# Attention on one core: the first K load cut in two parts on two DMA queues

## The chip, the cores and the metric

The kernel runs on one core of one Trainium2 chip. The metric is the device time of one execution in microseconds. In these runs the profiled span is about 1.7 us shorter than the time (823.1 beside 824.83 us).

## The reference

```python
B, H, Sq, Sk, D = 16, 32, 192, 1024, 128          # bf16
def reference(q, k, v):
    scale = q.shape[-1] ** -0.5
    scores = jnp.einsum("bhqd,bhkd->bhqk", q, k) * scale
    p = softmax(scores, axis=-1)
    return jnp.einsum("bhqk,bhkd->bhqd", p, v)
```

There are 512 heads. The inputs are 293.6 MB, the output 25.2 MB.

## The kernel before

The kernel takes four heads at a time: 128 groups, three pieces each. K of a group (1 MB) is loaded with 32 keys in each partition, "turned" by VectorE (32x32 transposes), put in order by GpSimd, and used by TensorE (PE) as the stationary operand of the scores. ScalarE takes the exponential; PE multiplies with V; VectorE divides. PE's program is a loop over two groups. K, V and Q have five buffers each, so at the start five K loads can be issued without waiting.

```python
PIECES = ((0, 6), (6, 12), (12, 16))      # which key blocks are in piece 0, 1, 2

@block.sync
def _(e):
    def load_k(x):
        if x >= NKN:
            e.wait_ge(s_kx, 3 * (x - NKN) + 3)
        e.dma_start(kn[:, x % NKN, :],
                    kf[4*x:4*x+4].rearrange("a (j r) d -> (a j) (r d)", r=32).bitcast(U32),
        ).then_inc(s_kn[x % NKN], 16)
    # ... load_v alike
    load_k(0)
    load_k(1)
    load_q(e, 1)
    for n in range(2, NKN):
        load_v(n - 2)
        load_k(n)
        load_q(e, n)
    # ... then as buffers come free

# VectorE
def turn_k(g):                            # piece g = 3 * x + b
    x, b = divmod(g, 3)
    lo, hi = PIECES[b]
    if b == 0:
        dve.wait_ge(s_kn[x % NKN], 16 * (x // NKN + 1))
    # ... transposes kn[.., lo:hi] into kx
turn_k(0)
turn_q(0)
for g in range(1, 5):
    turn_k(g)
turn_q(1)
# ...

# ScalarE
load_q(act, 0)
act.wait_ge(s_one, 1)
act.activation(pt[:, 1] ...)              # a fill that PE waits for before its loop
# ...
```

A piece is a range of key blocks `lo:hi` inside each of four stretches of a partition's row. Piece 0 is therefore 4 stretches of 768 bytes in each partition (384 KB), and the other keys of the group are 4 stretches of 1280 bytes (640 KB).

Of the kernel before, what the change touches and what calls it, by code (L numbers as in the profile page):

```python
# [407 lines left out]
U32 = mybir.dt.uint32  # L408
# [7 lines left out]
PIECES = ((0, 6), (6, 12), (12, 16))  # L416


def _attention_kernel(nc, q, k, v, out):
# [25 lines left out]
    with ExitStack() as outer:  # L445
        redo = outer.enter_context(nc.sbuf_tensor("redo", [1, 1], mybir.dt.int32))

        def sem(name):
            return outer.enter_context(nc.semaphore(name))

        s_set = sem("f_set")
        s_one = sem("f_one")
        s_kn = [sem("f_kn%d" % i) for i in range(NKN)]
        s_qn = [sem("f_qn%d" % i) for i in range(NKN)]
        s_v = [sem("f_v%d" % i) for i in range(NVS)]
# [16 lines left out]
        with ExitStack() as es:  # L472
# [49 lines left out]
            def load_q(e, x):  # L522
                e.dma_start(
                    qn[:, x % NKN, :],
                    qf[4 * x:4 * x + 4].rearrange("a (j u) d -> (a j) (u d)", u=6).bitcast(U32),
                ).then_inc(s_qn[x % NKN], 16)

            hints = {}

            def hint(eng):  # L530
# [2 lines left out]
# [5 lines that stand above are left out]
                    e.dma_start(  # L538
                        kn[:, x % NKN, :],
                        kf[4 * x:4 * x + 4].rearrange("a (j r) d -> (a j) (r d)", r=32).bitcast(U32),  # L540
                    ).then_inc(s_kn[x % NKN], 16)

                def load_v(x):
                    if x >= NVS:
                        e.wait_ge(s_pv, 3 * (x - NVS) + 2 + BLANK)
                    e.dma_start(
                        vs[:, x % NVS, :, :],
                        vf[4 * x:4 * x + 4].rearrange("a (m t) d -> m a (t d)", t=T),
                    ).then_inc(s_v[x % NVS], 16)

                load_k(0)
                load_k(1)
                load_q(e, 1)
                for n in range(2, NKN):
# [3 lines that stand above are left out]
                for n in range(NQ):  # L558
                    if n == NQ // 2:
                        hint(e)  # L560
                    if n + NKN - 2 < NQ:
                        load_v(n + NKN - 2)
                    if n + NKN < NQ:
                        load_k(n + NKN)
                        load_q(e, n + NKN)
                for i in range(len(store_at), len(stores)):
                    store(e, i)
# [125 lines left out]
            @block.vector  # L693
            def _(dve):
                dve.memset(pt[:, 0].rearrange("p a c -> p (a c)").bitcast(U32), 0).then_inc(s_set, 1)  # L695
                dve.sem_inc(s_e1, 1)
                dve.sem_inc(s_e3, 3)
                dve.sem_inc(s_vp, 2)
                dve.sem_inc(s_on, LAG + 1)
                where = {}  # L700
                for i, (x0, c) in enumerate(stores):
                    for a in range(c):
                        where[x0 + a] = (i, a)

                def turn_k(g):
                    x, b = divmod(g, 3)
                    lo, hi = PIECES[b]
                    if b == 0:
                        dve.wait_ge(s_kn[x % NKN], 16 * (x // NKN + 1))
                    if x >= 2:  # L710
                        dve.wait_ge(s_qk, 3 * (x - 2) + b + 1)
                    dve.transpose(  # L712
                        kx[:, x % 2].rearrange("p (U s j u) -> p s u U j", s=2, j=32, u=2)[:, :, :, lo:hi],
                        kn[:, x % NKN].rearrange("p (s u U i) -> p s u U i", s=2, u=2, i=32)[:, :, :, lo:hi],
                    ).then_inc(s_kx, 1)

                def turn_q(x):
                    dve.wait_ge(s_qn[x % NKN], 16 * (x // NKN + 1))
                    if x >= R:
                        dve.wait_ge(s_qk, 3 * (x - R) + 3)  # L720
                    dve.transpose(  # L721
                        qt[:, x % R].bitcast(U32).rearrange("p b (y j u) c -> p u y b (j c)", y=3, u=2),
                        qn[:, x % NKN].rearrange("p (u y b i) -> p u y b i", u=2, y=3, b=2),
                    ).then_inc(s_qt, 1)

                def onorm(s):
                    x, w = divmod(s, 3)
                    i, a = where[x]
                    so = i % NSO
                    ri = rinv[:, 2 * s: 2 * s + 2]  # L730
                    dve.wait_ge(s_pv, s + 1 + BLANK)
                    O = o_of(s)
                    dve.reciprocal(ri, O[:, :, 128]).then_inc(s_rc, 1)  # L733
                    dve.wait_ge(s_rc, s + 1)
                    if a == 0 and w == 0 and i >= NSO:
                        dve.wait_ge(s_st[so], 16 * (i // NSO))
                    dve.tensor_tensor(  # L737
                        ob[:, so, 6 * a + 2 * w: 6 * a + 2 * w + 2, :],
                        O[:, :, 0:128],
                        ri.unsqueeze(2).to_broadcast([128, 2, D]),  # L740
                        ALU.mult,
                    ).then_inc(s_on if s < NF - 1 else s_fin, 1)

                cnt = [0]

                def check(lo, hi, i, part):
                    c = chk[:, lo:hi]
                    if part == 0:
                        ins = dve.tensor_scalar(c, rinv[:, lo:hi], 1.0 / RS_HI, 1.0 / RS_LO, ALU.max, ALU.min)  # L749
                    elif part == 1:  # L750
                        ins = dve.tensor_tensor(c, c, rinv[:, lo:hi], ALU.not_equal)  # L751
                    else:
                        ins = dve.tensor_reduce(bad[:, i: i + 1], c, mybir.AxisListType.X, ALU.max)  # L753
                    ins.then_inc(s_dv, 1)
                    cnt[0] += 1
                    dve.wait_ge(s_dv, cnt[0])
# [6 lines that stand above are left out]
                for f in range(NF + LAG + 1):  # L763
                    s = f - LAG - 1
                    if f == NF // 2:
                        hint(dve)
                    if s >= 0:
                        onorm(s)
                        if 0 <= s - EARLY < 3:
                            check(0, 2 * EARLY, 0, s - EARLY)  # L770
                    g = f + 5
                    if g < NF:
                        x, b = divmod(g, 3)
                        if b == 2 and x >= 2:
                            turn_q(x)
                        turn_k(g)
                for part in range(3):
                    check(2 * EARLY, 2 * NF, 1, part)
                dve.sem_inc(s_fl, 1)  # L779
                dve.wait_ge(s_fl, 2)  # L780
                dve.tensor_copy(redo[0:1, 0:1], o_ps[0:1, 0, 0:1]).then_inc(s_fl, 1)  # L781
                dve.wait_ge(s_fl, 3)

            @block.scalar
            def _(act):
                load_q(act, 0)
                act.wait_ge(s_one, 1)
                act.activation(pt[:, 1].rearrange("p a c -> p (a c)").bitcast(F32), ones[:, 0:1].to_broadcast([128, 2 * T * SQ]),  # L788
                               ACT_FN.Copy).then_inc(s_set, 1)
                for f in range(NF):  # L790
                    x, b = divmod(f, 3)
                    if f == NF // 2:
                        hint(act)
                    act.wait_ge(s_qk, f + 1)
                    if 0 < 3 * x + b and b < 2:
                        act.wait_ge(s_pv, 3 * (x - R) + 2 + b + BLANK)
                    c = slice(512 * b, 512 * b + 512)
                    act.activation(pt[:, x % R, 0, c], s1_ps[:], ACT_FN.Exp, scale=scale).then_inc(s_e1, 1)  # L798
                    if b == 0:
                        act.wait_ge(s_pf, x + 1)  # L800
                    act.activation(pt[:, x % R, 1:4, c], s3_ps[f % 2][:], ACT_FN.Exp, scale=scale).then_inc(s_e3, 1)  # L801
                    if f in store_at:
                        store(act, store_at[f])
# [40 lines left out]
```

## Time and profile before

| | |
|---|---|
| Time, first three runs | 823.41 us median (823.04 to 824.85) |
| PE busy over the span | 98% |
| PE from 35 us to the end of the loop | busy (99.96 us of 100 from 200 us on, all of every other stretch), one group each 6.21 us |
| First scores | 8.62 us |
| DMA | 400 to 405 GB/s |

The first lines are the page's own: busy time of the engines, and two rows of the 40 slices (granted TensorE clock and DMA share in tenths).

```profile
PE 807.8 (98%) x32926; PEld 717.7 (87%) x32926; DVE 599.6 (73%) x1288; ACT 748.5 (91%) x770; POOL 549.6 (67%) x646
...
PEclk9899999999999999999999999999999999999999
DMA  9999999999999999999999999999999999999961
```

The next are two stretches of the table of windows (stretch, its length, busy time of each engine with its instructions, clock, DMA share, GB/s). They show that PE leaves no gap in the steady part. A change of the start can therefore only move this steady part as a whole.

```profile
60.00:100.00 40.00, 40.00 (x1642) 35.71 (x1644) 29.84 (x64) 37.42 (x40) 27.34 (x33) 1.00 1.04 405
400.00:500.00 100.00, 100.00 (x4126) 89.25 (x4120) 74.73 (x161) 93.63 (x98) 68.23 (x81) 1.00 1.04 401
```

The timeline of the start follows: start, duration, engine, line, operation, count, and in brackets the engine's idle time and what ended it. It shows the chain from the load to the first scores (6.43, 7.47, 8.62), and then three stalls of PE inside runs of matmuls where the program has no wait (2.41, 3.06 and 2.12 us; "issue" means that the profile shows nothing that PE waited for).

```profile
0.80 0.40 ACTq L523 DMA_DIRECT2D f_qn<-in_q_dram  x1
...
0.81 0.89 SPq L538 DMA_DIRECT2D f_kn<-in_k_dram  x2
...
6.43 0.98 DVE L712 STREAM_TRANSPOSE f_kx<-f_kn 128x768 uint32<-128x768 uint32 x1 [2.29 <-DMA f_kn<-in_k_dram]
7.33 0.54 DVE L721 STREAM_TRANSPOSE f_qt<-f_qn 128x384 uint32<-128x384 uint32 x1
...
7.47 0.85 POOL L583 COPY f_kt<-f_kx 128x768 uint32<-128x768 uint32 x1 [2.80 <-DVE f_kx L712]
...
8.62 1.10 PE L628 MATMUL f_s<-f_qt,f_kt 32*128 32x192 bf16 x48 [2.32 <-PEq L611]
...
15.49 0.98 PE L628 MATMUL f_s<-f_qt,f_kt 32*128 32x128 bf16 x40 [2.41 <-issue]
...
21.87 1.62 PE L650 MATMUL f_o<-f_vp,f_pt 128*64 128x129 bf16 x26 [3.06 <-issue]
...
28.46 1.89 PE L628 MATMUL f_s<-f_qt,f_kt 32*128 32x128 bf16 x46 [2.12 <-issue]
```

The last is the DMA view of 2.5 to 4.5 us, when the first loads are moved: queue, packets, MB, share of 16 engines. q1 is SyncE's queue (K), q10 ScalarE's (Q). A packet here is one contiguous run of a load, as the trace records it. There are nearly equal counts of 8 KB and 1.5 KB packets: the two queues take turns. (The records don't name the DMA engine of a packet, so this is read from the counts.)

```profile
DMA packets 145, 0.68 MB, mean 341 GB/s; under 512 B 0, under 2 KB 76, under 8 KB 76
...
q1 hardware_dynamic: 69, 0.57, 68.8%
q10 hardware_dynamic: 76, 0.12, 22.9%
```

### The profile page before, as it was taken

How to read it: one execution, taken by the hardware profiler on the slowest of the kernel's cores; microseconds unless marked ns; L12 is line 12 of the kernel's file. 1: busy time of each engine (PE TensorE's matmuls, PEld its weight loads, DVE VectorE, ACT ScalarE, POOL GpSimd, SP SyncE). 2: the span in 40 equal slices, each digit the busy share in tenths (PEclk: the TensorE clock that was granted, in tenths of full speed). 3: DMA queues.
4: the chain of work that ended last, by engine and by line, in shares of the span. 5: the costliest groups of instructions: out<-in, count | busy, mean ns of one | idle time of the engine just before them, and what ended most of it. 6: DMA issues, size and time to landing. Idle time of an engine off the chain costs nothing. (4 is left out here: it accounts for less than half of the span.)

```text
span 823.1 us, 71558 instructions
## 1 busy us (share of the span) xinstructions
PE 807.8 (98%) x32926; PEld 717.7 (87%) x32926; DVE 599.6 (73%) x1288; ACT 748.5 (91%) x770; POOL 549.6 (67%) x646
## 2 busy tenths in 40 slices
PE   6899999999999999999999999999999999999998
PEld 4788888888888888888888888888888888888887
DVE  5477777777777777777777777777777777777775
ACT  5699999999999999999999999999999999999996
POOL 6466676676676666767667667667666666766762
PEclk9899999999999999999999999999999999999999
DMA  9999999999999999999999999999999999999961
GB/s 355 401 403 406 407 403 407 403 402 404 405 401 394 405 402 402 402 401 391 406 403 399 404 404 394 404 405 397 400 407 395 403 400 402 401 405 401 399 226 59
DMA packets 138293, 319.14 MB, mean 388 GB/s; under 512 B 7184, under 2 KB 56336, under 8 KB 121872
## 3 DMA queue, kind: packets, MB, share of 16 engines
q1 hardware_dynamic: 105376, 294.22, 91.3%
q10 hardware_dynamic: 32880, 24.58, 8.9%
q14 instruction: 32, 0.26, 0.1%
q8 instruction: 5, 0.08, 0.0%
HBM read 293.60 MB, written 25.17 MB: 387 GB/s over the span
## 5 line engine op out<-in xcount | busy, mean ns | idle before, releaser
L801 ACT ACTIVATE f_pt<-f_s 128x1536 bf16<-128x1536 f32 x384 | 554.9, 1445 | 3.2 <-PE f_o L650 3.2
L583 POOL COPY f_kt<-f_kx 128x768 uint32<-128x768 uint32 (+1 forms) x384 | 293.5, 784 | 254.4 <-DVE f_kx L712 134.2
L628 PE MATMUL f_s<-f_qt,f_kt 32*128 32x192 bf16 (+2 forms) x20480 | 422.9, 226 | 6.9 <-issue 4.5
L650 PE MATMUL f_o<-f_vp,f_pt 128*64 128x129 bf16 x12336 | 424.7, 222 | 3.3 <-issue 3.3
L650 PEld LDWEIGHTS f_o<-f_vp,f_pt 128*64 128x64 bf16 x12336 | 365.2, 110 | 54.3 <-issue 24.8
L628 PEld LDWEIGHTS f_s<-f_qt,f_kt 32*128 32x128 bf16 x20480 | 348.2, 92 | 43.2 <-issue 7.4
L712 DVE STREAM_TRANSPOSE f_kx<-f_kn 128x768 uint32<-128x768 uint32 (+1 forms) x384 | 334.1, 871 | 8.7 <-DMA f_kn<-in_k_dram 8.7
L798 ACT ACTIVATE f_pt<-f_s 128x512 bf16<-128x512 f32 x384 | 229.2, 597 | 63.1 <-PE f_s L628 32.9
L592 POOL COPY f_vp<-f_vs 128x1024 uint32<-128x1024 uint32 x256 | 259.1, 1040 | 8.4 <-PE f_o L650 8.4
L733 DVE RECIPROCAL f_rinv<-f_o 128x2 f32<-128x2 f32 x381 | 64.8, 170 | 195.9 <-PE f_o L650 195.9
L737 DVE TENSOR_TENSOR f_ob<-f_o,f_rinv 128x256 bf16<-128x256 f32 x381 | 161.6, 424 | 13.3 <-DVE f_rinv L733 0.3
L721 DVE STREAM_TRANSPOSE f_qt<-f_qn 128x384 uint32<-128x384 uint32 x128 | 72.8, 569 | 0.0
L675 PE MATMUL f_o<-f_ones 128*128 128x512 bf16 x12 | 4.4, 540 | 1.1 <-POOL f_ones L574 1.1
L675 PEld LDWEIGHTS f_o<-f_ones 128*128 128x128 bf16 x12 | 1.5, 131 | 3.5 <-issue 2.2
L575 POOL MEMSET f_vp<- 128x4352 uint32 x1 | 3.7, 3728 | 0.0
L695 DVE MEMSET f_pt<- 128x3072 uint32 x1 | 2.6, 2618 | 1.5 <-PEq L829 1.5
L650 PE MATMUL f_s<-f_vp,f_pt 128*64 128x129 bf16 x96 | 3.1, 220 | 0.4 <-PEq L611 0.4
L650 PEld LDWEIGHTS f_s<-f_vp,f_pt 128*64 128x64 bf16 x96 | 2.8, 110 | 0.5 <-issue 0.5
L788 ACT ACTIVATE f_pt<-f_ones 128x3072 f32<-128x3072 bf16 x1 | 2.8, 2762 | 0.0
L788 ACT ACT_TABLE_LOAD x1 | 1.3, 1283 | 1.2 <-PEq L829 1.2
L733 DVE RECIPROCAL f_rinv<-f_s 128x2 f32<-128x2 f32 x3 | 0.5, 171 | 1.4 <-PE f_s L650 1.4
L689 PE MATMUL f_o<-f_bad,f_ones 128*1 128x1 bf16 x1 | 0.2, 164 | 1.3 <-DVEq L779 1.3
(13 smaller groups left out, 5.3 us busy)
## 6 DMA issues: line engine op xcount, KB each, us to landing
f_kn<-in_k_dram SPq DMA_DIRECT2D x128, 1024.0 KB, 10.6
f_vs<-in_v_dram SPq DMA_DIRECT2D x128, 1024.0 KB, 8.4
f_qn<-in_q_dram SPq DMA_DIRECT2D x127, 192.0 KB, 10.5
out_dram<-f_ob ACTq DMA_DIRECT2D x62, 384.0 KB, 9.5
out_dram<-f_ob SPq DMA_DIRECT2D x1, 384.0 KB, 3.2
out_dram<-f_ob SPq DMA_DIRECT2D x2, 192.0 KB, 2.3
f_qn<-in_q_dram ACTq DMA_DIRECT2D x1, 192.0 KB, 5.0
```

The source lines that it names most:

```text
L583: gp.tensor_copy(kt[:, x % NKT].bitcast(U32).rearrange("p U (j s u) c -> p U j s (u c)", s=2, u=2)[:, lo:hi], kx[:, x % 2].rearrange("p (U ...
L592: gp.tensor_copy(vp[:, x % NVP, 2 * T * i: 2 * T * i + 2 * T, 0:D].bitcast(U32), vs[:, x % NVS, 2 * i: 2 * i + 2, :].rearrange("p a (t d) ...
L628: ins = pe.matmul(S[:, c0: c0 + n1 - n0], kt[r, x % NKT, 2 * t + h, :, c], qt[r, x % R, h, n0:n1, c], start=w == 0 and g == 0, stop=w == 3 ...
L650: return pe.matmul(O[m0: m0 + m, u, 0:129], pt[:, x % R, 2 * y + z, t * SQ + n0: t * SQ + n0 + m], vp[:, x % NVP, (2 * y + z) * T + t, 0:129],
L675: pe.matmul(o_ps[:].rearrange("p a b -> p (a b)"), ones[:], ones[:].unsqueeze(1).to_broadcast([128, 4, 128]), start=True, stop=True)
L712: dve.transpose(kx[:, x % 2].rearrange("p (U s j u) -> p s u U j", s=2, j=32, u=2)[:, :, :, lo:hi], kn[:, x % NKN].rearrange("p (s u U i) ...
L721: dve.transpose(qt[:, x % R].bitcast(U32).rearrange("p b (y j u) c -> p u y b (j c)", y=3, u=2), qn[:, x % NKN].rearrange("p (u y b i) -> ...
L733: dve.reciprocal(ri, O[:, :, 128]).then_inc(s_rc, 1)
L737: dve.tensor_tensor(ob[:, so, 6 * a + 2 * w: 6 * a + 2 * w + 2, :], O[:, :, 0:128], ri.unsqueeze(2).to_broadcast([128, 2, D]), ALU.mult,). ...
L788: act.activation(pt[:, 1].rearrange("p a c -> p (a c)").bitcast(F32), ones[:, 0:1].to_broadcast([128, 2 * T * SQ]), ACT_FN.Copy).then_inc( ...
L798: act.activation(pt[:, x % R, 0, c], s1_ps[:], ACT_FN.Exp, scale=scale).then_inc(s_e1, 1)
L801: act.activation(pt[:, x % R, 1:4, c], s3_ps[f % 2][:], ACT_FN.Exp, scale=scale).then_inc(s_e3, 1)
```

## The change

VectorE's first turn needs only the keys of piece 0, but waits for the whole megabyte. The change loads these keys separately on SyncE's queue, with the first Q behind them, and the other keys on ScalarE's queue, where the first Q was. The intent is that piece 0 lands sooner.

```diff
+        s_k0 = sem("f_k0")
+            k0 = kf[0:4].rearrange("a (j s t) d -> (a j) s (t d)", s=4, t=8).bitcast(U32)
+            kn0 = kn[:, 0].rearrange("p (s w) -> p s w", s=4)
+            cut = 32 * PIECES[0][1]
@@ SyncE
-                load_k(0)
+                e.dma_start(kn0[:, :, 0:cut], k0[:, :, 0:cut]).then_inc(s_k0, 16)
+                load_q(e, 0)
                 load_k(1)
                 load_q(e, 1)
@@ VectorE, turn_k
-                    if b == 0:
+                    if g == 0:
+                        dve.wait_ge(s_k0, 16)
+                    elif g == 1 or b == 0:
                         dve.wait_ge(s_kn[x % NKN], 16 * (x // NKN + 1))
@@ ScalarE
-                load_q(act, 0)
+                act.dma_start(kn0[:, :, cut:], k0[:, :, cut:]).then_inc(s_kn[0], 16)
```

## The prediction

> # Prediction
>
> **What bounds the kernel.** From about 30 us on, TensorE: the table of windows has PE busy 100.00 of 100 us in every later stretch at clock 1.00, and the timeline repeats every 6.21 us for each of the 128 groups of four heads (795 us). DMA is nearly full beside it (400 to 405 GB/s), but SyncE's queue waits for PE (view of waits: 581 us), and VectorE waits for K data only three times, 8.7 us, all before 22 us. Only the start and the end can give time; the end is untouched.
>
> **The start** (timeline). Both first loads are issued at 0.8 us; K lands at 6.4, Q at 5.8. VectorE turns piece 0 (6.43, 0.98 us), GpSimd orders it (7.47, 0.85 us), the first score matmuls start at 8.62. This chain is critical. Then PE stalls three times inside runs of matmuls, with no wait of the program: 13.08 to 15.49, 18.82 to 21.87, 26.34 to 28.46. I read these as instruction fetches: the packet records have 16384-byte packets of a queue of its own from 13.0, 19.35 and 25.9 us (0.9 to 1.1 us each), and PE goes on 1.5 us after each. [...] here the stalls lie about 250 instructions apart. Each later fetch starts about 4 us after PE went on with the block before, so I take the chain to hang on PE's progress: if PE starts x earlier, all of it moves x, and so does the steady state.
>
> **What the change does.** No byte is removed. The first K load, 128 packets of 8 KB (309 ns each), becomes 512 packets of 768 B on SyncE's queue (384 KB) and 512 of 1280 B on ScalarE's (640 KB); Q's 192 KB moves behind the first. Piece 0 no longer waits for the other keys. In the packet records the two queues alternate packet by packet (17 to 21 of each in 0.5 us while both are live). [...] So SyncE's 32 packets per engine alternate with ScalarE's 32, and the 384 KB land nearly with the other 640: 1.0 MB comes first in place of 1.24. At 405 GB/s that saves 0.5 us; a split equal by bytes would save about 1.1. Against it: small packets are less efficient (768 B took 36 to 38 ns, 8 KB 309; estimate 0.3 us over 1 MB)[...]. I expect piece 0 at about 5.9 us. Q follows within 0.5 us, before VectorE wants it. Piece 1 lands with piece 0; PE's second piece had 1 us of slack.
>
> **Time.** 823.4 - 0.5 = 822.9 us. Noise beside it: two clock windows of 3.4 us at half speed (from 21.4 and 28.3 us) may fall otherwise, worth up to 1 us, and the three runs before spread over 1.8 us. Range 821.5 to 824.4. Faster by over 2%: 0.005; within 2%: 0.99; slower: 0.005.
>
> **What would show it.** VectorE's first turn at 5.7 to 6.1; first score matmuls 0.3 to 0.8 us earlier; three stalls still there, shifted with them; period 6.21 us; same bytes. Wrong if: the first turn is not earlier (small packets eat it) or 1 us earlier (queues share by bytes); the fetches do not move with PE's start, so the stalls swallow the gain; VectorE then waits for Q or piece 1; or the half-clock windows cost or give a microsecond.

The forecast's sum came to 823.4 - 0.5 = 822.9 us. In the trace of the kernel before, the first 16 packets of each queue took 62 to 847 ns.

## The result

The changed kernel took 824.87 us median (824.57 to 825.61, 4 runs), the kernel before 824.13 us (823.04 to 825.24, 4 runs, the first three included). The ratio is 1.001, 95% interval 0.9993 to 1.0028. A ratio is the mean time of one kernel's fast runs over that of the other's of the same rounds, so it is not quite the ratio of the medians quoted. The time lies 0.47 us above the predicted range, and the predicted gain did not appear.

The steady part of the changed kernel is the same, as the page and the window show.

```profile
PE 810.1 (98%) x32926; PEld 718.8 (87%) x32926; DVE 599.5 (73%) x1288; ACT 748.6 (91%) x770; POOL 550.7 (67%) x646
...
PEclk9899999999999999999999999999999999999999
DMA  8999999999999999999999999999999999999961
```

```profile
60.00:100.00 40.00, 40.00 (x1664) 35.57 (x1654) 29.96 (x65) 37.35 (x40) 27.54 (x32) 1.00 1.04 405
400.00:500.00 100.00, 100.00 (x4130) 89.12 (x4120) 74.86 (x162) 93.56 (x98) 68.34 (x80) 1.00 1.04 401
```

The timeline of the start shows what is different. The first turn starts at 6.80 us instead of 6.43, and the first scores at 8.99 instead of 8.62. PE goes on after the three stalls at 15.89, 22.55 and 29.02 us: 0.40, 0.68 and 0.56 later.

```profile
0.81 0.68 SPq L557 DMA_DIRECT2D f_kn<-in_k_dram  x1
0.81 0.65 ACTq L795 DMA_DIRECT2D f_kn<-in_k_dram  x1
...
6.80 0.98 DVE L721 STREAM_TRANSPOSE f_kx<-f_kn 128x768 uint32<-128x768 uint32 x1 [2.66 <-DMA f_kn<-in_k_dram]
7.70 0.54 DVE L730 STREAM_TRANSPOSE f_qt<-f_qn 128x384 uint32<-128x384 uint32 x1
7.84 0.85 POOL L590 COPY f_kt<-f_kx 128x768 uint32<-128x768 uint32 x1 [3.16 <-DVE f_kx L721]
...
8.99 1.15 PE L635 MATMUL f_s<-f_qt,f_kt 32*128 32x192 bf16 x48 [1.98 <-PEq L618]
...
15.89 0.99 PE L635 MATMUL f_s<-f_qt,f_kt 32*128 32x128 bf16 x40 [0.99 <-issue]
...
22.55 0.93 PE L657 MATMUL f_o<-f_vp,f_pt 128*64 128x129 bf16 x26 [3.32 <-issue]
...
29.02 1.08 PE L635 MATMUL f_s<-f_qt,f_kt 32*128 32x128 bf16 x46 [1.76 <-issue]
```

The DMA view of the same 2 us shows why the turn is late. Only q10, ScalarE's queue, moves anything, and it moves keys that nobody waits for yet. The two queues no longer take turns. They moved 0.47 MB in these 2 us, against 0.68 before.

```profile
DMA packets 365, 0.47 MB, mean 234 GB/s; under 512 B 0, under 2 KB 365, under 8 KB 365
...
q10 hardware_dynamic: 365, 0.47, 62.8%
```

Counted from the trace's packet records (packets that start in each 0.5 us, by queue and size):

```
us          before: q1 8192 B / q10 1536 B    changed: q10 1280 B / q1 768 B
2.0 to 2.5           7 / 20                            16 /   0
2.5 to 3.0           9 / 17                             7 /   0
3.0 to 3.5          18 / 18                            52 /   0
3.5 to 4.0          21 / 20                           151 /   0
4.0 to 4.5          21 / 21                           155 /   0
4.5 to 5.0          23 / 17                           119 /  55
5.0 to 5.5          26 /  1                            12 / 218
5.5 to 6.0          26 /  0                             0 / 211
```

By the semaphore records ScalarE's part had landed at 5.74 us, and piece 0 at 6.78 us.

### The profile page after: what moved, and what is told of

It reads as the page before. It is cut to its first block, busy times and chain, and to the rows that moved or that the text cites. A ratio compares the mean times of both kernels' runs of the same rounds, so it can differ in the third digit from the quotient of the medians.

```text
span 823.4 us, 71559 instructions
## 1 busy us (share of the span) xinstructions
PE 810.1 (98%) x32926; PEld 718.8 (87%) x32926; DVE 599.5 (73%) x1288; ACT 748.6 (91%) x770; POOL 550.7 (67%) x646
```

## The experiments

All kernels gave the right result. Four numbers of each trace are put side by side: the start of VectorE's first turn, of the first and the second piece of scores, and of the 21st exponential of the first kind (128x512). The 21st is in the steady part, so it tells by how much the steady part is moved; it is called the settled part below. "Ratio" is to the kernel before in the same rounds.

| run | first turn | first scores | second scores | 21st exp. | median us (before) | ratio, 95% interval |
|---|---|---|---|---|---|---|
| before, first trace | 6.43 | 8.62 | 10.68 | 62.13 | | |
| b0_before | 6.62 | 8.82 | 12.44 | 62.31 | 824.69 (824.9) | 1.0000, 0.9987 to 1.0014 |
| changed, first trace | 6.80 | 8.99 | 11.95 | 62.74 | 824.87 (824.13) | 1.0010, 0.9993 to 1.0028 |
| e0_after | 6.59 | 8.79 | 11.80 | 62.55 | 825.31 (823.23) | 1.0017, 1.0003 to 1.0031 |
| e13_after_again | 6.79 | 8.98 | 12.04 | 62.90 | 825.83 (825.19) | 1.0002, 0.9987 to 1.0017 |
| e1_swap | 4.71 | 8.78 | 12.25 | 62.49 | 824.74 (823.23) | 1.0012, 0.9998 to 1.0025 |
| e2_one_queue | 4.61 | 6.81 | 11.21 | 60.88 | 823.58 (823.23) | 1.0000, 0.9986 to 1.0014 |
| e3_scalar_later | 4.67 | 8.10 | 10.15 | 62.26 | 824.27 (823.23) | 1.0002, 0.9988 to 1.0015 |
| e4_q_on_scalar | 4.53 | 7.04 | 11.07 | 61.19 | 823.4 (824.9) | 0.9987, 0.9971 to 1.0003 |
| e5_late_turn | 8.93 | 11.06 | 14.77 | 63.73 | 827.14 (824.9) | 1.0035, 1.0020 to 1.0050 |
| e6_whole_rows | 5.82 | 8.02 | 10.08 | 60.55 | 823.45 (824.9) | 0.9990, 0.9977 to 1.0003 |
| e7_q_first | 4.91 | 7.11 | 12.89 | 62.00 | 825.16 (824.7) | 1.0013, 1.0000 to 1.0027 |
| e8_q_behind | 5.86 | 8.05 | 10.11 | 63.78 | 824.18 (824.7) | 0.9995, 0.9981 to 1.0008 |
| e9_swap_q_first | 10.29 | 12.48 | 16.19 | 65.72 | 828.45, one run | |
| e10_half_rows | 6.44 | 8.64 | 10.70 | 63.25 | 825.46, one run | |
| e11_hold_k1 | 4.82 | 7.01 | 9.46 | 60.36 | 824.31 (825.19) | 0.9995, 0.9979 to 1.0011 |
| e12_paced | 4.54 | 7.01 | 9.07 | 70.91 | 834.63 (825.19) | 1.0119, 1.0103 to 1.0135 |
| e14_two_held | 4.68 | 6.91 | 9.59 | 58.25 | 822.11 (824.68) | 0.9976, 0.9962 to 0.9989 |

### How much is chance: b0_before, e0_after, e13_after_again

The kernel before against itself (no edit):

> The kernel before against itself, to see what chance does to the start and the time. Theory: same first turn (6.3 to 6.5 us) and first scores (8.5 to 8.8), but the free-lying clock windows of 3.4 us and the instruction fetches move the settled part by up to 1.7 us between runs; ratio 0.999 to 1.001, runs 822.8 to 825. If the kernel before is the same in every run, the spread of 2 us seen so far must come from elsewhere and all runs here lie within 0.5 us.

The ratio was 1.0000, but its six runs spread from 823.24 to 825.61 us. The five sets of runs of the kernel before have medians of 823.23, 824.9, 824.7, 825.19 and 824.68 us. So the 823.41 us that the prediction started from was at the low end of what this kernel does. Its traces give one reason that can be seen. The trace's clock records have windows of half speed, 3.41 us long or a multiple of that (the stretches at full speed between or before them in the first traces of the two kernels are 3.41, 10.24 and 17.07 us), and they lie elsewhere in each run: from 21.43 and 28.26 us in the first trace, and from 8.88, 22.54 and 29.36 us in this one, where the second piece of scores is 1.76 us later for it. What sets their place is not shown. The runs before with the higher mean clock were mostly the shorter ones (in one set 822.77 to 823.23 us at 0.995 to 0.998, against 824.46 to 824.91 us, three of four at 0.992 to 0.994), but not all.

The traces allow a sum that goes further. Take the time at which PE goes on after its last stall of this kind (28.46 us in the first trace, 28.62 in b0_before). From there to the settled part it is 32.19 to 32.22 us in the four traces in which no half-speed window falls between (e5, e6, e9, e14), 33.6 to 33.8 us where 3.0 to 3.4 us of half speed do, and 34.7 and 34.9 us where 5.6 and 6.2 us do (e10 and e8); only e12, with more waits after that stall, is left out. So by these traces a microsecond at half speed there costs about 0.44 us, and a window of 3.41 us about 1.5. From the settled part to the end of the span all 18 traces take 760.4 to 761.1 us. So the traces differ by two things: when PE goes on after that stall, and how much half speed follows. That the untraced runs spread for the same reasons is likely, but not shown. A trace is of one run, and in e5, e6, e7, e11, e12 and e14 that run was the fastest of its set, so a settled part is to be read beside the ratio.

The changed kernel again, twice (no edit to it):

> The changed kernel again, for more runs and a second trace. Theory A (on every DMA engine ScalarE's packets of the first load, which piece 0 doesn't need, are moved before SyncE's): ScalarE's 640 KB land about 1 us before SyncE's 384 KB again (first trace: 5.74 and 6.78 us), the first turn starts at 6.7 to 6.9 us, first scores near 9.0, ratio to before 1.0003 to 1.0010. If the order of the two queues is chance, this trace shows it otherwise, or both landing together.

> The changed kernel a third time. If it is really slower by what its late first turn and the settled part show (0.2 to 0.6 us): ratio 1.0002 to 1.0017 once more, first turn 6.5 to 6.9, ScalarE's packets through before SyncE's. If the two are equal and the earlier ratios were chance: ratio 0.9990 to 1.0002.

In all three traces ScalarE's packets went first, and piece 0 landed at 6.78, 6.57 and 6.77 us. The mean first turn is 6.73 us against 6.53 in the two traces of the kernel before; the mean settled part is 62.73 against 62.22 us, so 0.5 us later. The half-speed windows don't explain it: PE goes on after the third stall 0.45 us later (28.99 against 28.54 us on average), with 3.41 us of half speed after it in all three traces, against 3.21 and 3.41. The three ratios are 1.0010, 1.0017 and 1.0002; one of the three intervals excludes 1. The changed kernel is not faster. That it is slower, by about 0.1%, is likely from traces and ratios together, but not firmly shown by the times.

### Is the order of the queues the cause: e1_swap, e2_one_queue, e3_scalar_later, e9_swap_q_first

Theory: on the DMA engines the 512 packets of the load that comes first are moved before the other queue's. Rivals: small packets are slow on any queue, or the queue with the larger packets goes first.

```diff
 e1_swap
-  SyncE: piece 0, Q;  ScalarE: other keys
+  SyncE: other keys;  ScalarE: piece 0, Q
 e2_one_queue
+  SyncE: piece 0, Q, other keys;  ScalarE: no load
 e3_scalar_later
+                act.wait_ge(s_one, 1)      # set near 1.0 us
                 act.dma_start(kn0[:, :, cut:], k0[:, :, cut:]).then_inc(s_kn[0], 16)
```

> The two queues swapped: piece 0's 384 KB and Q on ScalarE's, the other keys on SyncE's; same packets. Theory A (ScalarE's packets go first at the start): piece 0 lands at 4.2 to 5.0 us, first turn before 5.1, first scores 1.2 to 1.7 us earlier than before (near 7.1), time 0.5 to 2 us under before (ratio 0.9975 to 0.9995). Rival B (packets of 768 B are just slow at the start, on either queue): first turn still at 6.3 or later, ratio 1.000 or above. Rival C (the queue with the larger packets goes first): SyncE's 1280-byte packets go first, first turn at 6.3 or later.

> All on SyncE's queue, in the order piece 0, Q, other keys; none on ScalarE's. Theory A (what matters is who is in front on the engines): piece 0 lands at 4.5 to 5.2 us, first turn before 5.3, first scores near 7.3, ratio 0.9975 to 0.9998. Rival B (small packets are slow): first turn at 6.0 or later, ratio 1.000 or above.

> The changed kernel, but ScalarE issues its part only after a semaphore that is set near 1.0 us, so about 0.25 us after SyncE's issue. Theory A1 (first come, first served): SyncE's 768-byte packets now go first, piece 0 lands at 4.5 to 5.5 us, ratio 0.9975 to 0.9998. Theory A2 (ScalarE's queue has preference whenever it has packets): ScalarE's packets still finish first, piece 0 lands at 6.8 to 7.2, ratio above 1.0003. Sharing packet by packet, as predicted: both land together near 6.3.

In all three piece 0 landed at 4.59 to 4.69 us, 2 us sooner than in the changed kernel, with the same packets. So small packets as such don't make it late, and the larger packets don't win. In e3 only ScalarE's issue was put off by about 0.25 us, and the order turned round: SyncE's 768-byte packets started at 2.26 us and ScalarE's first only at 3.56 us. That is first come, first served.

The times however did not follow. The timeline of e3 (VectorE and PE lines) shows where the 2 us went: VectorE has piece 0 at 4.67 us and then waits 1.42 us for Q, which now lies behind piece 0 and shares the engines with the other keys.

```profile
4.67 0.98 DVE L721 STREAM_TRANSPOSE f_kx<-f_kn 128x768 uint32<-128x768 uint32 x1 [0.54 <-DMA f_kn<-in_k_dram]
...
7.07 0.58 DVE L730 STREAM_TRANSPOSE f_qt<-f_qn 128x384 uint32<-128x384 uint32 x1 [1.42 <-DMA f_qn<-in_q_dram]
...
8.10 1.09 PE L635 MATMUL f_s<-f_qt,f_kt 32*128 32x192 bf16 x48 [1.31 <-PEq L618]
```

In e1 Q held VectorE up to 7.75 us (a wait of 2.06 us), and the first scores came at 8.78. In e2 Q was in time and the first scores came at 6.81, but the other keys landed at 8.98 us, and the second scores waited for them until 11.21. The expected times were missed in all three (ratios 1.0012, 1.0000 and 1.0002).

A second test of first come: Q first on ScalarE's queue, piece 0 behind it, other keys on SyncE's.

> As the swapped run, but Q is first on ScalarE's queue and piece 0 behind it, so piece 0 is issued about 0.4 us after SyncE's other keys. First come, first served: SyncE's 1280-byte packets now go ahead and piece 0 lands last, at 5.7 to 6.9 us, although it is on the queue that won in the changed kernel. If ScalarE's queue wins by itself: piece 0 lands by 5.0 us.

SyncE's 1280-byte packets now went first (all but 3 of 512 had started by 5.0 us) and piece 0 came last, on the queue that had won in the changed kernel. So it is not ScalarE's queue that always wins, but the load that comes first. In the changed kernel the two loads are issued within 5 ns of each other, and ScalarE's was moved first in all three traces, and in e1 too; why it wins that tie is open. e3 and e9 show that it loses when it is issued 0.23 or 0.43 us later. Piece 0 landed far later than expected, at 10.27 us. In the packet records its 768-byte packets ran beside the next K load's 8 KB packets from 5.4 us on (17 or 18 of them in each 0.5 us from 6.5 to 8.0 us, against 201 from 5.0 to 5.5); the next experiments test what this does.

### Getting Q and the other keys in time too: e4_q_on_scalar, e7_q_first, e11_hold_k1

```diff
 e4_q_on_scalar
+  SyncE: piece 0, other keys, next K ...;  ScalarE: Q
 e7_q_first
+  SyncE: piece 0, next K ...;              ScalarE: Q, other keys
 e11_hold_k1   (as e7, and)
+                e.wait_ge(s_k0, 16)        # piece 0 has landed
                 load_k(1)
                 load_q(e, 1)
```

> Piece 0 then the other keys, both on SyncE's queue, Q alone on ScalarE's as before. Theory (order of arrival is all that the change is about): piece 0 lands at 4.6 to 5.3 us and Q by 5.3, other keys by 6.8, so first scores at 6.8 to 7.3 (1.3 to 1.8 us before the kernel before) and no wait of the second piece; the settled part is 0.5 to 1.8 us earlier, ratio 0.9978 to 0.9995. Rival (the fetches or the clock windows set the settled part, not the first scores): ratio 0.9995 to 1.001 with the first scores early all the same.

> The changed kernel, but Q goes ahead of the other keys on ScalarE's queue (as it was first there before the change) instead of behind piece 0 on SyncE's. Theory (first come: piece 0 on SyncE's queue arrives before the other keys, which ScalarE issues about 0.4 us later): Q and piece 0 land by 5.0 us, the other keys by 6.8, so the first turn starts before 5.1, first scores at 6.7 to 7.1 (limited by ScalarE's start fill), no wait of the second piece; settled part about 1.5 us before the kernel before, ratio 0.9970 to 0.9993, and 1.5 to 2.5 us under the changed kernel. If the start is not what sets the time, ratio 0.9995 to 1.0005.

First scores came early in both, at 7.04 and 7.11 us. But the other keys landed at 8.77 and 10.66 us instead of 6.8, so the second piece waited. The timeline of e7:

```profile
4.91 0.98 DVE L720 STREAM_TRANSPOSE f_kx<-f_kn 128x768 uint32<-128x768 uint32 x1 [0.77 <-DMA f_kn<-in_k_dram]
...
10.69 3.29 DVE L720 STREAM_TRANSPOSE f_kx<-f_kn 128x768 uint32<-128x768 uint32 x4 [4.34 <-DMA f_kn<-in_k_dram]
...
12.89 1.90 PE L634 MATMUL f_s<-f_qt,f_kt 32*128 32x192 bf16 x64 [3.66 <-PEq L617]
```

The packet records of e7 show the next K load's 8 KB packets beside the small ones: 15 or 16 of 8192 B with 32 to 52 of 1280 B in each 0.5 us from 4.5 to 6.0 us. The time of the engines went to the large packets (330 to 370 ns each on average, median 309, against 55 to 61). The test of that reading holds the next K load back until piece 0 has landed:

> As the run with Q first on ScalarE's queue, but SyncE issues the second K load (8 KB packets) only once piece 0 has landed, near 4.7 us. Theory (the other keys landed at 10.66 us because their 1280-byte packets took turns with 8 KB packets): they now land by 6.8 us, the first turn starts by 5.1, first scores near 7.1, no wait of the second piece (second score matmuls near 9.2 instead of 12.9); settled part 1 to 2 us before the kernel before, ratio 0.9970 to 0.9993. Rival (the last of the small packets lag for a reason of their own): other keys at 8.5 or later, ratio 0.9995 to 1.0015.

The other keys landed at 7.23 us instead of 10.66 (expected by 6.8), and the second scores started at 9.46 instead of 12.89. So the 8 KB packets beside them were indeed what delayed the small ones. The settled part of this trace is 1.8 us before that of the first trace of the kernel before, but its run was the fastest of six (822.67 to 827.07 us), and the ratio was 0.9995: the early start is not carried to the time reliably.

```profile
7.25 1.57 DVE L721 STREAM_TRANSPOSE f_kx<-f_kn 128x768 uint32<-128x768 uint32 x2 [1.00 <-DMA f_kn<-in_k_dram]
...
9.46 1.09 PE L635 MATMUL f_s<-f_qt,f_kt 32*128 32x192 bf16 x64 [0.32 <-PEq L618]
```

### The size of the packets: e8_q_behind, e6_whole_rows, e10_half_rows

These have the same 1 MB of K ahead of the first turn, with Q behind it, in packets of other sizes. In e6 and e10 the first turn waits for both parts, because their cut is not that of piece 0.

```diff
 e8_q_behind     one load of 8192 B packets, SyncE: K, Q;  ScalarE: no load
 e6_whole_rows   parts in one stretch a partition:   3072 B and 5120 B,  8 + 8 packets an engine
 e10_half_rows   parts in two stretches a partition: 1536 B and 2560 B, 16 + 16 packets an engine
 (changed)       parts in four stretches:             768 B and 1280 B, 32 + 32 packets an engine
```

> Only one thing of the change: K stays one load of 8 KB packets, Q is moved from ScalarE's queue to SyncE's, behind K; ScalarE issues no load. It measures the term that the prediction counted (192 KB less ahead of piece 0): K lands at 5.7 to 6.1 instead of 6.4, first scores 0.3 to 0.7 us earlier, ratio 0.9990 to 1.0002. If the start of SyncE's queue is slow alone, K lands at 6.3 or later.

> The changed kernel's two queues and sizes (384 KB on SyncE's, then Q; 640 KB on ScalarE's), but each part in whole stretches of a partition's row: 8 packets an engine of 3072 B and of 5120 B in place of 32 of 768 B and 32 of 1280 B; the first turn waits for both parts. If it is the many packets of one load that keep an engine for one queue, the packets of the two queues alternate here as they did before the change, and both parts land within 0.4 us of each other near 6.0. If first come is served out whatever the packets, ScalarE's 5120-byte packets are through before SyncE's start. First turn 5.9 to 6.5, ratio 0.9995 to 1.001 either way.

> As the run with whole stretches, but in two stretches a partition: 16 packets an engine of 1536 B and 16 of 2560 B; the first turn waits for both parts. It looks for the size at which the queues stop alternating. If alternation depends on packets of 2 KB or more, or on how many there are, these are served queue after queue or in a mix; if only the 768 and 1280-byte case is special, they alternate one by one (equal counts in every 0.5 us) and both land by 6.0.

The last byte of K landed at 5.84 us with 8192-byte packets, 5.80 with 3072 and 5120, 6.42 with 1536 and 2560, and 6.57 to 6.78 with 768 and 1280. So with Q out of the way K lands where the prediction had put it, but only in large packets. Cutting the same megabyte into the changed kernel's packets costs 0.87 us (mean landing 6.71 less 5.84). About half of this is in the packets' durations: 512 of 36 ns and 512 of 55 ns (medians) are 2.91 us for 16 engines, 128 of 309 ns are 2.47, an estimate of 0.44 us. The rest is in the start: between 2.5 and 4.5 us e6 moved 0.73 MB with its engines 92% busy, the changed kernel 0.47 MB with 63%. The first line is e8's first turn; the DMA view of e6 for these 2 us, below it, also shows the queues taking turns again, with 88 and 92 packets:

```profile
5.86 0.98 DVE L713 STREAM_TRANSPOSE f_kx<-f_kn 128x768 uint32<-128x768 uint32 x1 [1.73 <-DMA f_kn<-in_k_dram]
...
DMA packets 180, 0.73 MB, mean 367 GB/s; under 512 B 0, under 2 KB 0, under 8 KB 180
...
q10 hardware_dynamic: 88, 0.45, 56.7%
q1 hardware_dynamic: 92, 0.28, 34.9%
```

In e10 only ScalarE's queue moved packets in these 2 us (220 of 2560 B), as in the changed kernel. So taking turns was lost between 8 and 16 packets an engine for each load. Whether the number, the size or the stretched form of the load is what matters is open, because the three changed together here; and e7 shows that small packets do mix with 8 KB ones. The times of e8 (ratio 0.9995) and e6 (0.9990) do not contradict the predicted 0.5 us, but both intervals hold 1. Their traces don't show it carried through: both start the scores some 0.6 us earlier than the first trace before, but e8's PE went on after the first stall no earlier (15.49 us), and e6's no earlier after the second (21.83 us, against 21.87). After the last stall they went on at 28.84 and 28.34 us, against 28.46 and 28.62 in the two traces before. What sets their settled parts so far apart (63.78 and 60.55 us) is half speed after that stall, 6.2 us of it in e8 and none in e6. The traced run was the slowest of e8's set and the fastest of e6's.

### Is the start of PE carried to the end, and why does PE stall: e5_late_turn, e12_paced, e14_two_held

e5 puts a fill of 2.06 us between the landing of K and the first turn of the kernel before:

```diff
                     if b == 0:
                         dve.wait_ge(s_kn[x % NKN], 16 * (x // NKN + 1))
+                    if g == 0:
+                        dve.memset(idle[:], 0)      # 128 x 2400 words
```

> The kernel before with a fill of 2400 words on VectorE (about 2.0 us at the 0.85 ns a word of its start fill) between K's landing and the first turn: first scores 2.0 us later, loads as before. Theory (the start of PE is carried to the end): settled part and time 1.5 to 2.7 us later, ratio 1.0018 to 1.0033. Rival (fetches and DMA absorb it): under 0.7 us later, ratio under 1.0009.

The first turn was 2.3 to 2.5 us later than in the two traces of the kernel before, the settled part 1.4 to 1.6 us, and the time by the ratio 1.0035, about 2.9 us (interval 1.6 to 4.1). The settled part is the smaller because no half speed falls after the last stall of this trace; PE went on from that stall at 31.54 us, 2.9 to 3.1 us later. A late start is carried to the end, within the noise.

The prediction read the three stalls as instruction fetches, that is, as PE waiting until its next instructions are loaded. This is a reading; what the records show is the order in time. In the packet records a queue of its own (q8, of the kind that the DMA view names "instruction") moves one 16384-byte packet, in 0.88 to 1.10 us, before PE goes on from each stall, 1.3 to 1.5 us after the packet's end:

```
                 packet starts, us        packet ends              PE goes on
before        13.03  19.35  25.91     13.95  20.37  27.01     15.49  21.87  28.46
changed       13.41  20.01  26.52     14.43  21.03  27.62     15.89  22.55  29.02
e12_paced      9.34  13.06  20.15     10.22  14.04  21.17     11.73  15.38  22.56
```

A fourth such packet, at 32.09 us in the kernel before, came without a stall.

If these fetches are slow only because the DMA engines are full, issuing the next loads later must shorten the stalls. e12 is e11 with the next loads paced by PE's progress:

```diff
-                for n in range(2, NKN):
+                for n, (fv, fk) in zip(range(2, NKN), ((1, 3), (4, 6), (7, 8))):
+                    e.wait_ge(s_qk, fv)             # pieces of scores done
                     load_v(n - 2)
+                    e.wait_ge(s_qk, fk)
                     load_k(n)
                     load_q(e, n)
```

> The run before this one, and the next loads (V of group 0, K and Q of group 2, and so on up to group 4) are each issued only when PE has finished a named piece, so the DMA engines are not full in the first 20 us. Theory (the fetches wait in full DMA engines): from entering a block to going on takes 2 to 4 us instead of about 6.3, the three stalls of 2.1 to 3.1 us shrink to under 1 us each, settled part 4 to 9 us before the kernel before, ratio 0.989 to 0.996. Rival (a fetch takes 6 us by itself): stalls as before, ratio as the run before this one or worse. If the pace is too slow, VectorE or GpSimd waits for loads show in the first 40 us and eat the gain.

The first two lines are e11's, the others e12's:

```profile
13.62 0.98 PE L635 MATMUL f_s<-f_qt,f_kt 32*128 32x128 bf16 x40 [1.77 <-issue]
...
20.28 1.62 PE L657 MATMUL f_o<-f_vp,f_pt 128*64 128x129 bf16 x26 [3.33 <-issue]
...
11.73 0.98 PE L637 MATMUL f_s<-f_qt,f_kt 32*128 32x128 bf16 x40 [0.26 <-issue]
...
15.38 0.93 PE L659 MATMUL f_o<-f_vp,f_pt 128*64 128x129 bf16 x26 [0.31 <-issue]
...
22.56 1.08 PE L637 MATMUL f_s<-f_qt,f_kt 32*128 32x128 bf16 x46 [3.98 <-issue]
...
29.29 0.98 DVE L723 STREAM_TRANSPOSE f_kx<-f_kn 128x768 uint32<-128x768 uint32 x1 [8.67 <-DMA f_kn<-in_k_dram]
...
30.92 1.95 PE L659 MATMUL f_o<-f_vp,f_pt 128*64 128x129 bf16 x32 [7.28 <-PEq L620]
```

The first two stalls shrank from 1.77 and 3.33 us (e11) to 0.26 and 0.31 us. The second fetch started 1.33 us after PE had gone on with the block before (11.73 to 13.06), against 3.86 us in the kernel before (15.49 to 19.35). In the microsecond before that fetch the DMA engines were 69% busy, in the kernel before 96%. The third fetch is a check inside the same trace: with the engines full again it started 4.77 us after PE had gone on. So here the fetches started late when the DMA engines were full: this is shown, by one trace and the first stall of e14 below (0.39 us). What holds them up inside the DMA system is not. But the pace was too slow. The third stall, with loads under way again, was 3.98 us; then VectorE waited 8.67 us for the K load of group 3, which my pace issued only after the sixth piece of scores, and held up the outputs that PE waited for. The time was 1.2% worse.

e14 keeps the light start and frees the rest. V of group 0 is issued after the first piece, K of group 2 after the second, and then nothing is held; K of groups 3 and 4 goes ahead of V of groups 1 and 2:

```diff
+                e.wait_ge(s_qk, 1)
+                load_v(0)
+                e.wait_ge(s_qk, 2)
                 for n in range(2, NKN):
-                    load_v(n - 2)
                     load_k(n)
                     load_q(e, n)
+                    if n > 2:
+                        load_v(n - 2)
```

> As the run that holds the second K load, but V of group 0 is issued after the first piece of scores, K of group 2 after the second, and from there on nothing is held; K of groups 3 and 4 goes ahead of V of groups 1 and 2. Theory (the fetch chain sets the start): first two stalls under 1 us each as in the paced run, a third of 2 to 4 us, PE continuous from 24 to 28 us on, settled part 4 to 8 us before the kernel before, ratio 0.9900 to 0.9955. Rival (the loads bind instead): VectorE waits for K over 4 us before the tenth turn, settled part within 2 us of the run that holds the second K load, ratio 0.998 to 1.002 or worse.

In each stall's line below the bracket has its length; the line of VectorE (DVE) is the wait for K:

```profile
12.38 0.99 PE L639 MATMUL f_s<-f_qt,f_kt 32*128 32x128 bf16 x40 [0.39 <-issue]
...
19.27 1.62 PE L661 MATMUL f_o<-f_vp,f_pt 128*64 128x129 bf16 x26 [2.35 <-issue]
...
20.04 1.84 DVE L725 STREAM_TRANSPOSE f_kx<-f_kn 128x768 uint32<-128x768 uint32 x2 [4.38 <-DMA f_kn<-in_k_dram]
...
26.06 1.09 PE L639 MATMUL f_s<-f_qt,f_kt 32*128 32x128 bf16 x46 [1.25 <-issue]
```

The settled part is 3.9 us before that of the first trace of the kernel before, and the ratio is 0.9976 (0.9962 to 0.9989), about 2.0 us. Of the 3.9 us, 2.4 are PE's earlier going on after the third stall (26.06 against 28.46 us); the other 1.5 are that no half speed falls after it in this trace, the fastest of five runs. The gain is less than the theory's range: only the first stall became short, and VectorE waited 4.38 us for a K load in between. As the holding and the order of K and V were changed together, which of the two gives the gain is not shown. It is the only version here whose interval lies below 1, and it is faster than both kernels (the changed kernel has 1.0002 to 1.0017 to the same reference, in other rounds).

## Why the prediction was wrong

**What bounds the kernel** was right: the steady part is PE's in every trace, 6.21 us a group, and only the start moves.

**The order of the two queues** was wrong. The failing step reads: "So SyncE's 32 packets per engine alternate with ScalarE's 32, and the 384 KB land nearly with the other 640". They did not alternate. ScalarE's 512 packets were moved first, and piece 0 came last. By 4.5 us 381 of them had started, and none of SyncE's. The turns taken in the trace before were those of 8 packets an engine for each load, and I carried them over to 32; that they would go on there was my estimate, and no trace had shown it.

**The size of the gain** failed at another term. By volume this order alone costs nothing: 1.0 MB is ahead of the end of piece 0 whether the queues alternate or not, in place of 1.24 MB. e8 shows that term by itself: K landed at 5.84 us, as predicted ("about 5.9"). The mis-sized term is "small packets are less efficient (... estimate 0.3 us over 1 MB)". It measured 0.87 us: about 0.44 from the packet durations alone, and the rest from the slow start, which that figure did not include. And the prediction named its 0.3 us but did not take it off: its sum is 823.4 - 0.5. K landed at 6.41 and 6.59 us in the two traces before the change (mean 6.50; in e5, with the same loads, at 6.40). So the sum is -0.66 us for Q (6.50 to 5.84) and +0.87 us for small packets, together +0.2 us, where the prediction had -0.5. The prediction had listed this way to be wrong: "the first turn is not earlier (small packets eat it)". The term for Q rests on one trace of e8, and the landings of one kernel differ by 0.2 us between traces.

**The chain of fetches** was right in kind: in the changed kernel PE went on from the stalls 0.4 to 0.7 us later, after a first turn 0.37 us later, and e5 shows a delay carried to the end. But "if PE starts x earlier, all of it moves x" holds poorly the other way. e3, e7 and e11 started the scores 0.5 to 1.6 us earlier with ratios of 1.0002, 1.0013 and 0.9995, and in the traces of e6 and e8 a lead of 0.6 us in the scores was gone by the second stall. So even with piece 0 at 5.9 us the predicted gain in time was not assured. Q, the other keys, the fetches and the half-speed windows come next, and each takes part of the gain back.

**The noise** was under-rated. The range was built on three runs of 1.8 us spread around 823.41 us, and it took a half-speed window as worth up to 1 us, where the traces give about 1.5; later sets of the same kernel have medians from 823.23 to 825.19. Even with a true gain of 0.5 us the changed kernel would have missed the range on the slowest of these sets (825.19 - 0.5 = 824.69, above 824.4). In its own rounds, beside 824.13 us, it would have met it.

**What stays open**: why the loads with 16 or 32 packets an engine are moved one after the other; why ScalarE's goes first when both are issued together; why small packets start so slowly; and whether the changed kernel's 0.1% is real.

## What to carry to other kernels

When two queues start together, look at the packet records of each and ask which load arrives first and in what packets. Here the split load put the part that nobody needed in front (it landed at 5.74 us, piece 0 at 6.78), and the small packets lost both at the start (1 MB landed at 6.71 us on average, in 8 KB packets at 5.84) and beside 8 KB packets of the next load (the other keys landed at 10.66 us in e7, at 7.23 with the next load held back). After advancing one input, check what ends the next wait (here Q, then the other keys, then the stalls read as instruction fetches), since only the last of them sets the time. At the start of this kernel the second fetch came 3.86 us after PE had gone on with the DMA engines 96% busy, and 1.33 us after it with 69% (e12). Issuing fewer loads early, with K ahead of V, was faster than issuing all at once by 0.24% in e14; which of the two gives it is not shown.
